# First batch of an attention and Fourier-mixing kernel: order of loads, turning, folds and normalising rearranged

## The chip, the cores and the metric

The kernel runs on one core of a Trainium2 chip. The metric is the device time of one execution in microseconds (us), read as the median of several runs; lower is better. A core has five engines that each work through their own list of instructions in order: PE (TensorE, the matrix multiplier), DVE (VectorE), ACT (ScalarE), POOL (GpSimd) and SP (SyncE, which here only issues DMA transfers). They wait for one another through semaphores.

## The reference

There are two stages in float32. The first is attention inside chunks of 64 positions; the second mixes the result with a two-dimensional Fourier transform, adds it to itself, normalises every position, and sends it through a two-layer perceptron.

```python
# q, k, v: (8, 8, 576, 64); chunks of 64 positions
scores = scale * np.matmul(q_c, k_c.transpose(0, 1, 2, 4, 3))
attn = softmax(scores)
out = np.matmul(attn, v_c)
x = out.transpose(0, 2, 1, 3).reshape(B, S, H * D)      # (8, 576, 512)
mixed = np.real(np.fft.fft(np.fft.fft(x, axis=1), axis=2))
u = x + mixed
un = (u - mean(u)) / np.sqrt(var(u) + 1e-06)
ch = np.maximum(un @ w_ch1, 0.0) @ w_ch2                # 512 -> 2048 -> 512
result = u + ch
```

The weights `w_ch1` and `w_ch2` arrive as float64 bits. They are turned into float32 by bit operations on the chip ("rounding" below).

## The kernel before

**Tiles.** A tile is 128 positions (two chunks) by 512 columns. Each batch has nine chunks: four tiles named LO 0, LO 1, HI 0, HI 1, and half a tile RE, which two batches share. LO tiles hold positions in reversed order and HI tiles their mirror images, so that a sum and a difference of a LO and a HI tile ("fold") halve the Fourier work. Batch 0 is worked alone at the start by `attention_early` and `fourier_early`. Later batches are worked as side work beside the matrix products of the perceptron, which run in groups of four tiles (`mlp`). The first group begins with `up_first`, whose first product is L1064; from there on PE has a steady supply. The order of instructions within an engine is the order in which the code is written (`tc.manual_schedule()`), so each queue can be read off the code.

**Loading.** `load(n)` queues q and k of tile n on SP (those of tile 0's k on ACT), as 128 or 256 KB DMAs. `load_v(n)` queues v in four DMAs of 64 KB: POOL for tiles 0 to 2 (half of tile 0 on ACT), SP for tiles 3 and 4. Then SP issues the token tables (ten DMAs, `token_tables`), two rows of the dimension tables, the first weight piece, the cosine and sine tables and the further weight pieces.

**Attention of batch 0.** For each tile PE turns q and k (`att_T`, four 128x128 transposes each through `turn`, L350), ACT copies them to SBUF (L380, L389), PE multiplies them (`att_S`, L401), DVE takes the maximum and subtracts it (`softmax`, L414, L416), ACT exponentiates (L427), PE turns the result (`att_P`) and ACT copies it (L433), PE multiplies by v (`att_V`, L451), and DVE divides by the row sums (L464 to L468). All the turns use two PSUM buffers named "pt". `shift_early` exchanges single rows between tiles: `shift_early(0)` on POOL (L491 to L493), `shift_early(1)` on ACT (L495 to L497). `fold(0,1)` and `fold(0,NM)`, that of RE, are POOL's; `fold(0,0)` is DVE's (L523 to L548 all are lines of `fold`).

**Fourier of batch 0.** PE multiplies the folded tiles pm by the token tables (z, L837, and single-row products mid, L840), in the order 1, 0, NM. ACT and DVE copy z to SBUF (L851 to L859), PE multiplies by the dimension tables (L876), DVE adds the result to the tiles and takes statistics (L900, L903, L655, L656). ACT makes the reciprocal root (L659 and L660, a logarithm and an exponential). `normed` normalises tiles 0 and 1 on ACT (L943 to L945) and 2 and 3 on DVE (L947). `turned` turns each (L350) and ACT copies it (L960). `columns(s)` forms the first part of the first four up products for tile s alone (L892).

**Rounding of the weights.** `round_weight(i)` starts piece i ("head": DVE L323 and L333, ACT L318, L321 and L315) and finishes piece i-1 ("tail": DVE L330, L331, L339). The first up products need piece 0, L1064 needs piece 1, and each further piece of four products needs the next. The argument `later` puts ACT's three steps on a list (`put_off`), to be written further down.

**Warming.** `keep_warm(k)` issues k matmuls of zeros on PE (L1280), 128x289 each.

Of the kernel before, what the change touches and what calls it, by code (L numbers as in the profile page):

```python
# [16 lines left out]
def kernel(  # L17
# [103 lines left out]
    for b in range(B):  # L121
        first.append(len(tiles))
        if b % 2 == 0:
            tiles.append((RE, b, 0))
        tiles += [(LO, 0, 1), (HI, 0, 1), (LO, 0, 0), (HI, 0, 0)] if b == 0 else [
            (what, b, i) for what in (LO, HI) for i in range(NM)
        ]
# [93 lines left out]
    def load_v(n):  # L221
        t = more_v[n - 3] if 3 <= n < first[1] else v_ring[n % 3]
        for i, (b, c) in enumerate(chunks(n)):
            for e in range(2):
                eng = nc.scalar if n == 0 and e else nc.gpsimd if n < 3 else nc.sync
# [8 lines left out]
    def token_tables(to):  # L234
# [5 lines left out]
        for c in range(2):  # L240
            j, p0 = divmod((NC - 1 - c) * CH, 128)
            for r in range(2):
                r0 = CH * c + CH // 2 * r
                nc.sync.dma_start(
# [3 lines left out]
        for r0 in (0, CH):  # L248
            nc.sync.dma_start(out=to[r0:r0 + CH // 2, NM], in_=seq_tab[1:CH:2, NM, :, 0:n])
            w = seq_tab.shape[1]  # L250
            lone = seq_tab.rearrange("p j r f -> (p j) r f")[0:2 * w + NM + 1:2 * w + NM]
            nc.sync.dma_start(out=to[r0 + CH // 2:r0 + CH // 2 + 2, NM], in_=lone[:, :, 0:n])
            nc.sync.dma_start(out=to[r0 + CH // 2 + 2:r0 + CH, NM], in_=seq_tab[4:CH:2, NM, :, 0:n])

    def load_tables():

        token_tables(early_tk)
        for i in range(2):
            nc.sync.dma_start(out=first_rest[32 + 32 * i:33 + 32 * i, 0:DM], in_=dim_tab[0:1, 1 + 2 * i, :])
# [86 lines left out]
    def turn(src):  # L346

        pt = ps_t.tile([128, 4, 128], FP32, tag="pt", name="pt")
# [5 lines left out]
    def att_T(n, which="qk"):  # L354
# [21 lines left out]
        a = qs.pop(n)  # L376
        pt = turn(lambda j: a[:, 2 * j:2 * j + 2, :].rearrange("p h d -> p (h d)"))
# [8 lines left out]
        a2 = ks.pop(n)  # L386
        pt = turn(lambda j: a2[:, 2 * j:2 * j + 2, :].rearrange("p h d -> p (h d)"))
# [3 lines left out]
        if first[1] <= n + 1 < NT:  # L391
            load(n + 1)
# [44 lines left out]

    def att_V(n):
        a, b = pT.pop(n), vs.pop(n)
# [7 lines left out]
        for j in range(NJ):  # L447
            for e in range(2):
                for c in range(2):
# [7 lines left out]
                    )  # L457
        x = xt(n)
# [19 lines left out]
        if kind(n) == HI:  # L478
            (nc.vector if n == at[HI, 0, 0] else nc.gpsimd).tensor_copy(x[:, 0:1], x[:, DM:DM + 1])
# [5 lines left out]
    def shift_early(i):  # L485
# [8 lines left out]
        else:  # L494
            nc.scalar.copy(rest, lows[0][r0])  # L495
            nc.scalar.copy(lows[0][r0], lows[0][r1])
            nc.scalar.copy(lows[0][r1], kept)  # L497
# [12 lines left out]
    def fold(b, i):  # L510

        eng = nc.vector if (b, i) == (0, 0) or b == 1 else nc.gpsimd
        if (b, i) == (0, 0):
            two = one_p.tile([128, KD, G * 128], FP32, tag="unT", name="two")
            two = two.rearrange("p k t -> p (k t)")[:, 0:2 * (HM + 1)]
        else:
            two = one_p.tile([128, 2 * (HM + 1)], FP32, tag="two", name="two")
        if i < NM:
# [3 lines left out]
            (nc.vector if (b, i) == (0, 0) else nc.gpsimd).memset(s[:, DM:DM + 1], 0.0)  # L522
# [13 lines left out]
        near, far = pmr[:, :, 0:HQ], pmr[:, :, HM:HQ:-1]  # L536
        if i < NM:
# [13 lines left out]
    def attention_early():  # L551
# [3 lines left out]
        def ready(n):  # L555
            if n == at[LO, 0, 1]:
                shift_early(0)
            if n == at[HI, 0, 1]:
                fold(0, 1)
            if n == at[HI, 0, 0]:  # L560
                fold(0, 0)
# [3 lines left out]
        att_T(lo)  # L565
        att_S(lo)
        for n in range(lo, hi + 1):
            if n < hi:
                att_T(n + 1)
            softmax(n)  # L570
            if n > lo:
                att_V(n - 1)
# [3 lines left out]
            if n in (lo, hi):  # L576
                keep_warm(1)
            att_P(n)
        shift_early(1)
        fold(0, NM)  # L580
        keep_warm(1)
        att_V(hi)
        ready(hi)
        keep_warm(6)
        round_weight(0)
        round_weight(1, parts="t")
# [231 lines left out]
    def fourier_early():  # L818
# [9 lines left out]
        mid = ps_f.tile([128, 512], FP32, tag="ff", name="mid")  # L828
        mids = [(CH * g + 1 if g else 0, CH * g + CH + 1 if g < 3 else NQ) for g in range(4)]
        order = (1, 0, NM)  # L830
# [29 lines left out]
        round_weight(1, put_off, "h")  # L860
# [20 lines left out]
        for do in put_off[:2]:  # L881
            do()
        keep_warm(3)
# [13 lines left out]
        for i in range(NM):  # L897
            y, (low, high) = early_xp[0][i], groups[0][2 * i:2 * i + 2]
            x = xt(low)
            nc.vector.tensor_tensor(out=x[:, 0:DM], in0=y, in1=x[:, 0:DM], op=ALU.add)  # L900
            means([low])
# [3 lines left out]
            if i == 0:  # L905
# [511 lines left out]
```

## Time and profile before

| | |
|---|---|
| median of 3 runs | 1079.0 us (1078.85 to 1080.7) |
| profiled execution | 1076.41 us |
| its span, first to last instruction | 1074.6 us |
| granted PE clock, mean | 1.000 |
| PE, DVE, ACT, POOL busy | 98%, 54%, 29%, 31% |
| PE busy in 0 to 10, 10 to 20, 20 to 30, 30 to 40, 40 to 50 us | 8.04, 8.29, 8.69, 9.77, 8.16 us |
| PE busy in 50 to 60, 60 to 70, 70 to 100 us | 10.00, 9.61, 30.00 us |
| share of DMA capacity in 0 to 20 us | 0.92 to 0.93 |
| scores' maximum (L414) of the five tiles starts at | 10.15, 12.90, 17.12, 20.52, 23.85 us |
| PE's waits before 55 us, the two longest sums | 1.8 us for ACT's copy of k, 1.6 us for ACT's normalising |

Times inside the execution count from the first instruction. PE's busy time includes the warming matmuls, so a high share in the first 50 us is not all work.

### The profile page before, as it was taken

Reading aid. Unit: us, or ns where it says so; the run is one execution under the profiler, and the core shown is the slowest. Engines: PE = TensorE matmul, PEld = TensorE weight load, DVE = VectorE, ACT = ScalarE, POOL = GpSimd, SP = SyncE. Lnnn points to the kernel's source line nnn. Section 1 sums busy time; section 2 is a strip of 40 time slices with the busy share of each in tenths; the row PEclk is TensorE's granted clock in tenths of the full one; section 3 lists DMA queues with packets and bytes.
Section 4 is the critical chain, followed back from the end, with each engine's and each line's share of the span. In section 5 each row is a group of like instructions: output and inputs, shape, how many; then the busy total and the mean of one; then the engine's idle time right before and its main releaser. Section 6 shows DMA issues by size and latency. Waiting matters only on the chain.

```text
span 1074.6 us, 19747 instructions
## 1 busy us (share of the span) xinstructions
PE 1054.5 (98%) x7418; PEld 840.0 (78%) x7418; DVE 578.6 (54%) x1269; ACT 311.6 (29%) x732; POOL 330.2 (31%) x475
## 2 busy tenths in 40 slices
PE   8999989999999999999999999999999999999998
PEld 6645444446888888888888888888888888888887
DVE  4798985324567465655565555745664434323411
ACT  4688563123113411323022312331133113101300
POOL 4311017573515240254124321624161401310140
PEclk9999999999999999999999999999999999999999
DMA  8767566598467546892678356945653355436232
GB/s 181 234 184 216 119 195 198 172 300 296 146 192 229 160 144 194 219 243 100 194 203 243 115 167 194 259 152 168 212 168 118 120 184 177 128 141 215 77 118 79
DMA packets 148780, 192.25 MB, mean 179 GB/s; under 512 B 68140, under 2 KB 105004, under 8 KB 141518
## 3 DMA queue, kind: packets, MB, share of 16 engines
q1 hardware_dynamic: 145036, 187.59, 57.8%
q10 hardware_dynamic: 3330, 2.76, 1.0%
q8 instruction: 59, 0.97, 0.4%
q0 software_dynamic: 320, 0.66, 0.3%
q14 instruction: 35, 0.29, 0.1%
HBM read 166.83 MB, written 24.12 MB: 178 GB/s over the span
## 4 chain that ended last, share of the span: by engine, by line
PE 78%; DMA 6%; DVE 4%; POOL 3%; ACT 3%; SPq 3%; issue 2%; POOLq 0%; DVEq 0%; ACTq 0%
PE pb L1200 21%; PE pa L1151 17%; PE pa L1200 16%; PE pb L1151 12%; PE up L1084 2%; PE pt L350 2%; PE up L1064 2%; DMA xall<-in_moe_w_ch_dram 2%; PE mix L791 2%; PE z L672 1%; DMA v<-in_v_dram 1%; PE xp L451 1%; SPq L216 1%; DMA q<-in_q_dram 1%; PE sc L401 1%
## 5 line engine op out<-in xcount | busy, mean ns | idle before, releaser
L1151 PE MATMUL pa<-unT,wa 128*128 128x256 f32 x672 | 159.9, 381 | 1.6 <-DVE wa L1159 1.6
L1151 PEld LDWEIGHTS pa<-unT,wa 128*128 128x128 f32 x672 | 126.2, 190 | 19.4 <-DVE wa L1159 2.0
L1052 POOL TENSOR_TENSOR h<-h 128x256 f32<-128x256 f32 x64 | 55.3, 871 | 231.2 <-DVE wb L1050 138.7
L1200 PE MATMUL pa<-wb,h 128*128 128x256 f32 x512 | 115.7, 380 | 0.0
L1200 PE MATMUL pb<-wb,h 128*128 128x256 f32 x512 | 114.9, 379 | 0.0
L1151 PE MATMUL pb<-wa 128*128 128x256 f32 x448 | 106.6, 381 | 0.0
L1200 PEld LDWEIGHTS pa<-wb,h 128*128 128x128 f32 x512 | 96.0, 190 | 13.0
L1200 PEld LDWEIGHTS pb<-wb,h 128*128 128x128 f32 x512 | 96.3, 190 | 12.6
L1151 PEld LDWEIGHTS pb<-wa 128*128 128x128 f32 x448 | 84.3, 190 | 11.5
L508 POOL COPY xall<-xall 1x512 f32<-1x512 f32 x28 | 17.8, 637 | 147.3 <-DVE xall L468 120.4
L1157 DVE TENSOR_TENSOR wa<-pb,wa 128x256 f32<-128x256 f32 x56 | 23.8, 424 | 69.9 <-ACT wa L1156 69.9
L1200 PE MATMUL pb<-wb,yall 128*128 128x256 f32 x256 | 58.2, 381 | 0.0
L1200 PE MATMUL pb<-wb 128*128 128x256 f32 x256 | 57.7, 379 | 0.0
L1200 PE MATMUL pa<-wb,yall 128*128 128x256 f32 x256 | 57.6, 379 | 0.0
L1105 PE MATMUL dn<-wb,h 128*128 128x512 f32 x128 | 57.5, 597 | 0.0
L1084 PE MATMUL up<-unT,wa 128*128 128x512 f32 x128 | 56.8, 595 | 0.0
L1156 ACT COPY wa<-pa 128x256 f32<-128x256 f32 x56 | 20.9, 372 | 124.0 <-PE pa L1151 81.2
L1151 PE MATMUL pa<-wa 128*128 128x256 f32 x224 | 53.9, 383 | 0.0
L1151 PE MATMUL pb<-unT,wa 128*128 128x256 f32 x224 | 52.9, 379 | 0.0
L1200 PEld LDWEIGHTS pa<-wb,yall 128*128 128x128 f32 x256 | 48.0, 190 | 6.1
L1200 PEld LDWEIGHTS pb<-wb,yall 128*128 128x128 f32 x256 | 47.7, 190 | 6.3
L1200 PEld LDWEIGHTS pb<-wb 128*128 128x128 f32 x256 | 47.6, 190 | 5.9
(265 smaller groups left out, 1766.8 us busy)
## 6 DMA issues: line engine op xcount, KB each, us to landing
wb<-s SPq DMA_DIRECT2D x56, 1024.0 KB
wa<-s SPq DMA_DIRECT2D x196, 256.0 KB
xall<-in_moe_w_ch_dram SPq DMA_DIRECT2D x22, 512.0 KB
q<-in_q_dram SPq DMA_DIRECT2D x96, 112.0 KB
k<-in_k_dram SPq DMA_DIRECT2D x96, 112.0 KB
v<-in_v_dram SPq DMA_DIRECT2D x124, 64.0 KB
yall<-in_moe_w_ch_dram SPq DMA_DIRECT2D x10, 512.0 KB
s<-wb SPq DMA_DIRECT2D x20, 256.0 KB
```

What stands on the lines that cost most here:

```text
L216: eng.dma_start(out=t[p0:p0 + np_], in_=src[b, :, c * CH:c * CH + np_, :].rearrange("h p d -> p h d"))
L350: nc.tensor.transpose(pt[:, j, :], src(j), ident)
L508: nc.gpsimd.tensor_copy(to, from_)
L791: nc.tensor.matmul(out=mix[:, cols], lhsT=zt[:, T], rhs=tab, start=(T == 0), stop=(T == 3), skip_group_check=True,)
L1052: nc.gpsimd.tensor_tensor(out=h1[:, m, hi], in0=h1[:, m, lo], in1=h1[:, m, hi], op=ALU.subtract)
L1064: nc.tensor.matmul(out=up, lhsT=w1[:, kk, m * 128:(m + 1) * 128], rhs=unT[:, kk], start=(kk == 0), stop=(kk == KD - 1), skip_group_check=True,
L1084: nc.tensor.matmul(out=up, lhsT=w1[:, kk, m * 128:(m + 1) * 128], rhs=unT[:, kk], start=(kk == 0), stop=(kk == KD - 1),)
L1105: nc.tensor.matmul(out=dn, lhsT=h1[:, m, s * 128:(s + 1) * 128], rhs=w2[:, m, :], start=(m == 0), stop=(m == KF - 1),)
L1151: nc.tensor.matmul(out=dst, lhsT=w[:, kk, r], rhs=rhs[o][:, kk], start=(o in (0, 1) and kk == 0), stop=(kk == 1), skip_group_check=True,)
L1156: nc.scalar.copy(a, dst)
L1157: nc.vector.tensor_tensor(out=b, in0=pbs[r][:, 0], in1=a, op=ALU.add)
L1200: nc.tensor.matmul(out=dst, lhsT=lhs[:, m], rhs=w[:, m], start=(o in (0, 2) and m == 0), stop=(m == HF - 1), skip_group_check=True,)
```

## The change

The tile order of batch 0 becomes RE, LO 1, LO 0, HI 1, HI 0. SP queues q and k of all five tiles, and then v of tiles 3 and 4. POOL queues v of tiles 0 to 2, the token tables and the two rows; a small copy that needs the first half of q of tile 0 stands before them. In the tile loop k is turned into a third PSUM bank ("bank") two tiles ahead and q into "pt", also issued by PE earlier (q three tiles ahead, k two), and ACT copies q before the exponentials' turn. `att_V` is split in products and scaling, and the scaling of tile n-1 is written behind the softmax of tile n. Both exchanges are POOL's, the first half of `fold(0,1)` is DVE's (with a buffer in `wb`) and its second half POOL's. `fold(0,NM)` comes before it. z is summed in the order NM, 1, 0. The tail of piece 0's rounding moves from before the copies of z to behind them, together with the head of piece 1. All four tiles are normalised on DVE, each directly followed by its turn and its columns. There are fewer warming matmuls.

```diff
@@ -122,7 +122,7 @@
             tiles.append((RE, b, 0))
-        tiles += [(LO, 0, 1), (HI, 0, 1), (LO, 0, 0), (HI, 0, 0)] if b == 0 else [
+        tiles += [(LO, 0, 1), (LO, 0, 0), (HI, 0, 1), (HI, 0, 0)] if b == 0 else [
             (what, b, i) for what in (LO, HI) for i in range(NM)
@@ -222,7 +222,7 @@
             for e in range(2):
-                eng = nc.scalar if n == 0 and e else nc.gpsimd if n < 3 else nc.sync
+                eng = nc.gpsimd if n < 3 else nc.sync
                 eng.dma_start(
@@ -241,22 +241,22 @@
                 r0 = CH * c + CH // 2 * r
-                nc.sync.dma_start(
+                nc.gpsimd.dma_start(
                     out=to[r0:r0 + CH // 2, 0:NM].rearrange("p i r f -> p (i r) f"),
...
         for r0 in (0, CH):
-            nc.sync.dma_start(out=to[r0:r0 + CH // 2, NM], in_=seq_tab[1:CH:2, NM, :, 0:n])
+            nc.gpsimd.dma_start(out=to[r0:r0 + CH // 2, NM], in_=seq_tab[1:CH:2, NM, :, 0:n])
             w = seq_tab.shape[1]
             lone = seq_tab.rearrange("p j r f -> (p j) r f")[0:2 * w + NM + 1:2 * w + NM]
-            nc.sync.dma_start(out=to[r0 + CH // 2:r0 + CH // 2 + 2, NM], in_=lone[:, :, 0:n])
-            nc.sync.dma_start(out=to[r0 + CH // 2 + 2:r0 + CH, NM], in_=seq_tab[4:CH:2, NM, :, 0:n])
+            nc.gpsimd.dma_start(out=to[r0 + CH // 2:r0 + CH // 2 + 2, NM], in_=lone[:, :, 0:n])
+            nc.gpsimd.dma_start(out=to[r0 + CH // 2 + 2:r0 + CH, NM], in_=seq_tab[4:CH:2, NM, :, 0:n])
...
         for i in range(2):
-            nc.sync.dma_start(out=first_rest[32 + 32 * i:33 + 32 * i, 0:DM], in_=dim_tab[0:1, 1 + 2 * i, :])
+            nc.gpsimd.dma_start(out=first_rest[32 + 32 * i:33 + 32 * i, 0:DM], in_=dim_tab[0:1, 1 + 2 * i, :])
@@ -343,9 +343,9 @@
-    def turn(src):
-
-        pt = ps_t.tile([128, 4, 128], FP32, tag="pt", name="pt")
+    def turn(src, pt=None):
+
+        pt = ps_t.tile([128, 4, 128], FP32, tag="pt", name="pt") if pt is None else pt
         for j in range(4):
@@ -373,8 +373,15 @@
             return
-        a = qs.pop(n)
-        pt = turn(lambda j: a[:, 2 * j:2 * j + 2, :].rearrange("p h d -> p (h d)"))
+        q_out(n, pair_turned(qs.pop(n)))
+        k_out(n, pair_turned(ks.pop(n)))
+        if first[1] <= n + 1 < NT:
+            load(n + 1)
+
+    def pair_turned(a, pt=None):
+        return turn(lambda j: a[:, 2 * j:2 * j + 2, :].rearrange("p h d -> p (h d)"), pt)
+
+    def q_out(n, pt):
         t = one_p.tile([128, 2 * NJ, CH + 1], FP32, tag="qT", name="qT")
@@ -383,13 +390,11 @@
         qT[n] = t
-        a2 = ks.pop(n)
-        pt = turn(lambda j: a2[:, 2 * j:2 * j + 2, :].rearrange("p h d -> p (h d)"))
+
+    def k_out(n, pt):
         t = one_p.tile([128, NJ, 128], FP32, tag="kT", name="kT")
...
         kT[n] = t.rearrange("p j (c t) -> p (j c) t", c=2)
-        if first[1] <= n + 1 < NT:
-            load(n + 1)
@@ -435,7 +440,13 @@
+    xps = {}
+
     def att_V(n):
+        att_V_products(n)
+        att_V_scaled(n)
+
+    def att_V_products(n):
         a, b = pT.pop(n), vs.pop(n)
@@ -455,6 +466,10 @@
                     )
+        xps[n] = xp
+
+    def att_V_scaled(n):
+        xp = xps.pop(n)
         x = xt(n)
@@ -476,7 +491,7 @@
         if kind(n) == HI:
-            (nc.vector if n == at[HI, 0, 0] else nc.gpsimd).tensor_copy(x[:, 0:1], x[:, DM:DM + 1])
+            (nc.vector if n < first[1] else nc.gpsimd).tensor_copy(x[:, 0:1], x[:, DM:DM + 1])
         elif kind(n) == RE:
@@ -492,9 +507,9 @@
         else:
-            nc.scalar.copy(rest, lows[0][r0])
-            nc.scalar.copy(lows[0][r0], lows[0][r1])
-            nc.scalar.copy(lows[0][r1], kept)
+            nc.gpsimd.tensor_copy(rest, lows[0][r0])
+            nc.gpsimd.tensor_copy(lows[0][r0], lows[0][r1])
+            nc.gpsimd.tensor_copy(lows[0][r1], kept)
@@ -509,17 +524,19 @@
-        eng = nc.vector if (b, i) == (0, 0) or b == 1 else nc.gpsimd
+        eng = nc.vector if b == 0 and i < NM or b == 1 else nc.gpsimd
         if (b, i) == (0, 0):
...
             two = two.rearrange("p k t -> p (k t)")[:, 0:2 * (HM + 1)]
+        elif (b, i) == (0, 1):
+            two = wb[:, 0:2 * (HM + 1)]
         else:
...
             low, high = xt(at[LO, b, i]), xt(at[HI, b, i])
-            (nc.vector if (b, i) == (0, 0) else nc.gpsimd).memset(s[:, DM:DM + 1], 0.0)
+            (nc.vector if b == 0 else nc.gpsimd).memset(s[:, DM:DM + 1], 0.0)
             eng.tensor_tensor(out=s[:, 0:DM], in0=low[:, 0:DM], in1=high[:, 0:DM], op=ALU.add)
@@ -534,6 +551,8 @@
         near, far = pmr[:, :, 0:HQ], pmr[:, :, HM:HQ:-1]
+        if (b, i) == (0, 1):
+            eng = nc.gpsimd
         if i < NM:
@@ -553,37 +572,52 @@
         def ready(n):
+            att_V_scaled(n)
             if n == at[LO, 0, 1]:
                 shift_early(0)
-            if n == at[HI, 0, 1]:
-                fold(0, 1)
-            if n == at[HI, 0, 0]:
-                fold(0, 0)
+            if n == at[LO, 0, 0]:
+                shift_early(1)
+                fold(0, NM)
+            for i in range(NM):
+                if n == at[HI, 0, i]:
+                    fold(0, i)
             if n + 3 > hi:
...
-        att_T(lo)
+        turned_q = {lo: pair_turned(qs.pop(lo))}
+        pair_turned(ks.pop(lo), bank)
+        q_out(lo, turned_q.pop(lo))
+        k_out(lo, bank)
         att_S(lo)
+        turned_q[lo + 1] = pair_turned(qs.pop(lo + 1))
+        pair_turned(ks.pop(lo + 1), bank)
+        q_out(lo + 1, turned_q.pop(lo + 1))
+        k_out(lo + 1, bank)
+        turned_q[lo + 2] = pair_turned(qs.pop(lo + 2))
         for n in range(lo, hi + 1):
-            if n < hi:
-                att_T(n + 1)
             softmax(n)
             if n > lo:
-                att_V(n - 1)
                 ready(n - 1)
...
                 att_S(n + 1)
-            if n in (lo, hi):
+            else:
                 keep_warm(1)
+            if n + 2 <= hi:
+                q_out(n + 2, turned_q.pop(n + 2))
             att_P(n)
-        shift_early(1)
-        fold(0, NM)
-        keep_warm(1)
-        att_V(hi)
+            if n + 2 <= hi:
+                pair_turned(ks.pop(n + 2), bank)
+                k_out(n + 2, bank)
+            else:
+                keep_warm(1)
+            if n + 3 <= hi:
+                turned_q[n + 3] = pair_turned(qs.pop(n + 3))
+            elif n + 3 == hi + 1:
+                load(hi + 1)
+            att_V_products(n)
         ready(hi)
-        keep_warm(6)
+        keep_warm(3)
         round_weight(0)
-        round_weight(1, parts="t")
@@ -825,9 +859,9 @@
         z += [more[:, k] for k in range(2)]
-        mid = ps_f.tile([128, 512], FP32, tag="ff", name="mid")
+        mid = bank.rearrange("p j t -> p (j t)")
         mids = [(CH * g + 1 if g else 0, CH * g + CH + 1 if g < 3 else NQ) for g in range(4)]
-        order = (1, 0, NM)
+        order = (NM, 1, 0)
         for i in order:
@@ -857,7 +891,7 @@
                 nc.scalar.copy(z4[0:1, 2, r:r + 1], chunk_order(from_))
-        round_weight(1, put_off, "h")
+        round_weight(1, put_off)
         to = zr[:, :, 0].rearrange("p t (r i) -> p t r i", r=2)
@@ -878,9 +912,7 @@
         idle[0] = mid
-        for do in put_off[:2]:
-            do()
-        keep_warm(3)
+        keep_warm(2)
         yield
@@ -898,27 +930,22 @@
             nc.vector.tensor_tensor(out=x[:, 0:DM], in0=y, in1=x[:, 0:DM], op=ALU.add)
+            if i == 1:
+                normed(0, 1)
+                turned(0, 1)
+                columns(1)
             means([low])
...
             nc.vector.tensor_tensor(out=x[:, DM:DM + 1], in0=y[:, 0:1], in1=x[:, DM:DM + 1], op=ALU.add)
-            if i == 0:
-                normed(0, 0)
-            if i == 1:
-                turned(0, 1)
-                columns(0)
+            normed(0, 2 * i)
+            turned(0, 2 * i)
+            columns(2 * i)
             means([high])
-            if i == 0:
-                normed(0, 1)
-                turned(0, 0)
-                keep_warm(1)
-        put_off[2]()
-        columns(1)
-        normed(0, 2)
-        turned(0, 2)
+            put_off.pop(0)()
+        put_off.pop(0)()
         normed(0, 3)
         turned(0, 3)
-        columns(2)
         columns(3)
@@ -938,7 +965,7 @@
         mean, rstd = sts.pop(n)
-        if g == 1 or g == 0 and s < 2:
+        if g == 1:
             shift_ = sm_p.tile([128, 1], FP32, tag="shift", name="shift")
@@ -1261,10 +1288,9 @@
             load(n)
-            if n < 3:
-                load_v(n)
-        load_v(3)
-        load_v(4)
+        nc.gpsimd.tensor_copy(zr[0:1, 0, 0, 0:1], start[0:1, 4 * DM:4 * DM + 1])
+        for n in range(first[1]):
+            load_v(n)
         load_tables()
@@ -1273,6 +1299,7 @@
         early_xp = [ps_f.tile([128, 512], FP32, tag="ff", name="early_xp") for _ in range(2)], None
+        bank = ps_f.tile([128, 4, 128], FP32, tag="ff", name="bank")
```

## The prediction

> **What bounds the kernel now.** I read busy shares first, then the table of windows, then the first 52 us engine by engine.
>
> ```profile
> PE 1054.5 (98%) x7418; PEld 840.0 (78%) x7418; DVE 578.6 (54%) x1269; ACT 311.6 (29%) x732; POOL 330.2 (31%) x475
> ```
> ```profile
> 10.00:20.00 10.00, 8.29 (x203) 6.59 (x195) 5.83 (x15) 6.40 (x13) 0.00 (x0) 1.00 0.93 192
> 40.00:50.00 10.00, 8.16 (x51) 6.46 (x50) 8.88 (x21) 8.95 (x31) 0.00 (x0) 1.00 0.57 132
> 50.00:60.00 10.00, 10.00 (x35) 5.30 (x35) 9.14 (x19) 8.48 (x14) 0.00 (x0) 1.00 0.77 239
> 70.00:100.00 30.00, 30.00 (x186) 15.35 (x185) 27.93 (x54) 25.44 (x44) 5.08 (x4) 1.00 0.72 203
> ```
> From 50 us on TensorE is full (30.00 of 30.00); before, it has gaps, and some of its work is warming matmuls. The change touches only what precedes the first product of `up_first` (L1064); after it, every engine has the same instructions in the same order. So the change is worth the shift of that one start, 51.49 us:
>
> ```profile
> 22.70 0.69 PE L401 MATMUL sc<-kT,qT 64*64 64x64 f32 x32
> 33.49 0.76 PE L837 MATMUL z<-wb,pm 128*128 128x289 f32 x2
> 37.09 0.34 PE L840 MATMUL mid<-wb,pm_rest 64*1 64x65 f32 x8
> 48.33 1.04 PE L350 MATMUL pt<-ident,un 128*128 128x128 f32 x8
> 51.49 1.88 PE L1064 MATMUL up_a<-unT,wa 128*128 128x512 f32 x4
> ```
> ```profile
> 23.85 0.68 DVE L414 TENSOR_REDUCE mx<-sc 128x8 f32<-128x512 f32 x1
> 29.61 1.23 DVE L523 TENSOR_TENSOR sum<-xall 128x512 f32<-128x512 f32 x1
> 33.25 0.16 DVE L548 TENSOR_TENSOR pm<-pm,sign 128x1 f32<-128x1 f32 x1
> 40.04 0.69 DVE L900 TENSOR_TENSOR xall<-early_xp,xall 128x512 f32<-128x512 f32 x1
> 47.74 0.55 DVE L947 TENSOR_SCALAR un<-xall,st,rstd 128x512 f32<-128x512 f32 x1 [0.35 <-ACT rstd L660]
> 50.08 0.68 DVE L339 TENSOR_TENSOR wa<-wa,power 128x512 f32<-128x512 f32 x1
> ```
> Start and length stand first; a bracket tells the wait. Milestones: last score maximum 23.85, last fold 33.41, z done 37.43, first residual add 40.04, last normalisation 48.29, first up product 51.49. Piece 1 of the weights (rounding ends L339, 50.76) is only 0.7 early, so VectorE is nearly as critical as TensorE.
>
> ```profile
> 20.75 0.60 POOL L491 COPY first_rest<-xall 1x512 f32<-1x512 f32 x1 [12.56 <-DVE xall L468]
> 28.76 0.72 POOL L530 TENSOR_TENSOR two<-xall 64x256 f32<-64x256 f32 x1
> 33.27 0.20 POOL L548 TENSOR_TENSOR pm_rest<-pm_rest,sign 64x1 f32<-64x1 f32 x1
> ```
> POOL idles 12.56 us before its first exchange, then folds (0,1) and (0,NM). Filling that idle is what the change tries with the table loads.
>
> **What the Trainium skill says.** "SBUF — State Buffer", section "SBUF: two separate sides": a DVE instruction with two SBUF inputs and a POOL instruction lock each other out of a shared port pair. The trace agrees: the fold's add took 1.23 us with POOL folding beside it, and the same add of the next batch, at 117.39 with POOL idle, 0.69. "DMA: Bandwidth & Descriptors", section "SWDGE vs HWDGE vs iDMA": GpSimd's and SyncE's DMAs feed different queues, between which an engine takes turns. The trace shows nothing against it: v loads from POOL landed by 12.8 us while q and k were still landing until 18.4. Its section "Anatomy of one DMA — SWDGE (gpsimd) path" gives 2.0 us plus bytes/436e3, an estimate of 2.15 us for 64 KB; the trace's median was 5.7 from issue to landing under load, and I use that. "TensorE: Matmul & The Clock Gate", Part 1: after an idle window of about 3.4 us the clock halves. Here PEclk stays 1.00; the first eight warming matmuls took 0.82 us and later ones 0.49.
>
> **The change, part by part.**
>
> *Tile loop.* Before, q, k and exponential share two "pt" buffers; the last three tiles are 3.3 us apart (17.12, 20.52, 23.85). With k in a third bank and q turned three tiles ahead, TensorE's own work remains, start to start: S 0.62, P 0.50, k 0.50, q 0.50, V 0.70 = 2.8 us; VectorE has 0.69+0.75+1.25 = 2.7. I take 2.7 to 2.9 for the last two distances, and 3.4 for that to the third tile (4.2 before, 12.90 to 17.12), which holds the first in-order V. Last maximum: 22.15 (−1.7). Bytes are unchanged, and DMA share is 0.93 here; tables now compete with q and k, so I put k of the last tile at 19 to 20 us (before 18.4), hardly late for its turn.
>
> *Folds.* Between the scaling of tiles 3 and 4, VectorE gains the first half of fold (0,1): 0.14+0.06+1.23+0.56+0.14+0.61 = 2.7, partly in its 1.44 us wait. From 22.15: maximum and subtraction 1.5, scaling 1.25, this 2.6, scaling 1.2, fold (0,0) 3.75 = 32.45 (−0.95).
>
> *POOL and the queues.* SyncE loses 12 table issues (4.9 us, 21.62 to 26.5), so weights start that much earlier; ACT loses two v issues. POOL gains a tiny copy that waits for the first half of q (4.41); behind it stand all v loads. The first of tile 0 then lands near 4.46+5.7 = 10.2, the last near 12 to 13, for a first V at about 14.5: hidden. POOL issues 12 v loads (0.62 each, from 4.46 after the copy that waits for q), then 10 table loads and 2 rows. With eight outstanding and 5.7 us to landing, 24 need three rounds: 4.46 + 16/8 × 5.7 + 8 × 0.55 = 20.3; I take 20.5, with 18 (SyncE's tables landed in 3 us) and 23 as ends. The last table lands some 4 us after its issue, 24 to 25, for a z that starts at 27.9: hidden up to 3 us. Behind the DMAs stand six exchanges at 0.68 (three were ACT's), fold (0,NM) 4.7 and half of fold (0,1) 1.9: done 31.4. ACT is relieved of 1.9 us, worth nothing: it was idle from 29.3 to 33.8.
>
> *z.* Order NM, 1, 0. At 20.5, (NM) runs from 27.9, (1) from 30.2, (0) from 32.8: done 35.2 (−2.2). But now the rest of piece 0's rounding and the start of piece 1's stand between the z copies and the first add: 0.33+0.60+0.61+0.33+0.60 = 2.5 us of VectorE; before, only L323 and L333 of piece 1, 0.77, stood there, and the others filled the wait for z. VectorE's two long and two short z copies, in turn with ACT's, end 1.2 after z (0.42+0.41+0.22+0.22, as from 37.85 to 39.35 before, less one wait): 36.4, plus 2.5 = first add 38.9 (−1.1). ACT's three steps on piece 0 (0.72+0.72+0.61 from 32.8) end at 34.85, when its first z copy can start; below z they cost nothing, and each 0.1 later would cost 0.1.
>
> *Normalising.* For tiles 0 and 1, ACT's 0.19+0.29+0.81 is replaced by 0.55 on VectorE. But the written order makes each tile a closed ring: normalise 0.55, turn 0.65, ACT copy 0.57, logarithm 0.33, exponential 0.23, plus hand-overs 0.1 = 2.43; the next tile's logarithm is queued on ACT behind the copy, which waits for TensorE. Add to first normalisation 2.2, three rings 7.3, the last 0.55: 10.1, against 8.25 before, where statistics ran ahead. Last normalisation: 48.99 (+0.7).
>
> *Tail.* Before 3.20 from there to L1064: two tiles' turns, copies and eight columns. Now one tile: 48.99 + turn 0.65 + copy 0.57 + columns 4×0.23 + hand-overs 0.2 = 51.3; piece 1's rounding takes 0.33+0.60+0.61+0.33+0.62 = 2.5, ready 51.48. First product 51.58 (−0.6).
>
> Sum: −1.1 + 1.8 − 0.6 = +0.1 us. The warming matmuls removed stood in idle; weights issued earlier by SyncE are not needed earlier. The profiled run was 1076.41 (span 1074.6 and 1.8 around it): 1076.5 becomes 1079.1 on the scale of the median 1079.0.
>
> **Rivals.**
>
> 1. Late POOL (slower). In the sum, POOL's done time and VectorE's fold meet at the start of z(0). Each microsecond by which POOL is free after 20.5 shifts everything: at 22.2 I get +1.9, at 23 about +2.8. From 22.6 on it decides "slower". For: DMA share 0.93, small table rows, software descriptors; against: SyncE needed only 4.3 us to issue all ten. Time: 1081.5.
> 2. The front counts in full (faster). VectorE's two fold adds meet POOL only exchanging rows and take 0.69 instead of 1.23 (1.1 less), POOL is free near 19, and the 1.8 us of piece 0's rounding (0.60+0.61+0.60) slip into waits for z as before (1.7 less): 0.1−2.8 = −2.7. For: both costs are avoidable ones, by the rows at 117.39 and 35.81. Against: in the written order that rounding comes after the copies. Time: 1076.3.
> 3. TensorE's clock falls. Between warming and the first turn some 2.5 us are empty; if the clock halves, three turns and columns take 0.5 to 1 us more each: +2. The gap is below the skill's window; PEclk never fell before. Time: 1081.
> 4. The order doesn't do what it says: q turned ahead stands in TensorE's queue before V, and waits for DMA; the loop keeps 3.3 us. Then the 1.7 gain is gone: +1.0, 1080.1, inside the range.
>
> **How the numbers follow.** About 2.2 us, 0.2%, can be told from no change. Balance near zero (with rival 4): 0.49. Rival 1: 0.23; rival 3: 0.08; rival 2: 0.20. So faster 0.20, same 0.49, slower 0.31. Likeliest time 1079.1; its own range is 1077.3 to 1080.8, and with POOL's ends and the rivals 1076.3 to 1082.3.
>
> **What would show it.** Right: last maximum near 22.2, last fold 32.5, first add 38.9, normalisations 2.4 apart on VectorE each waiting for ACT's exponential, first up product 51.6, later windows unchanged. POOL's first exchange after 22 shows rival 1; PEclk below 1.00 after 40 shows rival 3; a first add before 37.5 shows rival 2; maxima 3.3 apart show rival 4. I am wrong in kind if time moves after the first up product.

## The result, and the profile after

The changed kernel took 1087.76 us in the median of 4 runs (1086.27 to 1088.87), the kernel before 1079.83 us beside it (4 runs, 1078.85 to 1080.7): a ratio of 1.0073 with a 95% interval of 1.0053 to 1.0092. The profiled execution took 1086.27 us, with a span of 1084.5 us against 1074.6 before. It is slower, by about 8 us, where no measurable change was forecast. The profile of before is one of its quick executions, 1076.41 us, so the spans differ by 9.9 us and the medians by 7.9.

The table of windows (the columns are window, length, busy time of PE, PEld (TensorE's weight loads), DVE, ACT and POOL, granted PE clock, DMA share, GB/s; the view prints shares above 1 too):

```profile
10.00:20.00 10.00, 7.30 (x195) 6.10 (x194) 5.33 (x15) 6.45 (x14) 6.64 (x13) 1.00 1.22 220
40.00:50.00 10.00, 6.96 (x31) 5.35 (x29) 8.42 (x19) 4.13 (x21) 0.00 (x0) 0.79 0.43 108
50.00:60.00 10.00, 8.36 (x33) 7.27 (x34) 5.31 (x12) 6.02 (x14) 0.00 (x0) 0.50 0.17 52
70.00:100.00 30.00, 30.00 (x185) 15.44 (x184) 26.04 (x50) 26.14 (x44) 4.74 (x5) 1.00 0.64 172
```

The last column but two is what to read first: TensorE ran at half its clock from the middle of the 40s until past 60 us. The busy share hides it, because a matmul at half clock counts as busy for nearly twice as long. The timeline of PE shows where it began and what it did:

```profile
18.08 0.63 PE L350 MATMUL pt<-ident,start 128*128 128x128 f32 x4 [1.58 <-DMA start<-in_q_dram]
42.23 1.14 PE L1307 MATMUL bank<-warm 128*128 128x289 f32 x4
45.34 0.67 PE L350 MATMUL pt<-ident,un 128*128 128x128 f32 x4 [1.98 <-DVE un L974]
48.56 1.06 PE L350 MATMUL pt<-ident,un 128*128 128x128 f32 x4
59.38 3.62 PE L1091 MATMUL up_a<-unT,wa 128*128 128x512 f32 x4
```

The warming matmuls end at 43.36 us and the first normalised tile arrives 1.98 us later. The next turn takes 1.06 us instead of 0.67, and the first four up products (L1091, L1064 of before) 3.62 instead of 1.88. The whole start on DVE, and POOL's last load and first exchange:

```profile
23.23 0.68 DVE L419 TENSOR_REDUCE mx<-sc 128x8 f32<-128x512 f32 x1
26.24 0.24 DVE L479 TENSOR_SCALAR rd<-early_xp 128x4 f32<-128x4 f32 x2 [1.54 <-PE early_xp L462]
35.32 0.42 DVE L567 TENSOR_TENSOR pm<-pm,sign 128x1 f32<-128x1 f32 x1
42.42 0.69 DVE L932 TENSOR_TENSOR xall<-early_xp,xall 128x512 f32<-128x512 f32 x1
54.31 0.55 DVE L974 TENSOR_SCALAR un<-xall,st,rstd 128x512 f32<-128x512 f32 x1 [2.24 <-ACT rstd L694]
```
```profile
22.36 0.50 POOL L259 DMA_DIRECT2D first_rest<-in_dim_tab_dram  x1 [0.35 <-DMA wb<-in_seq_tab_dram]
23.02 0.60 POOL L506 COPY first_rest<-xall 1x512 f32<-1x512 f32 x1
```

The milestones, before and after: last maximum 23.85 and 23.23; POOL's first exchange 20.75 and 23.02; last fold ends 33.41 and 35.74; first add 40.04 and 42.42; first up product 51.49 and 59.38. So of the 9.9 us of span, 2.4 are lost up to the first add, 5.5 from there to the first up product (16.96 instead of 11.45), and 2.0 behind it; 1.7 of these are the first four products at half clock.

### The profile page after: what moved, and what is told of

It is laid out like the page before. It is cut to its first block, busy times and chain, and to the rows that moved or that the text cites. A ratio compares the mean times of both kernels' runs of the same rounds, so it can differ in the third digit from the quotient of the medians.

```text
span 1084.5 us, 19732 instructions
## 1 busy us (share of the span) xinstructions
PE 1060.4 (98%) x7408; PEld 844.1 (78%) x7408; DVE 582.0 (54%) x1277; ACT 308.0 (28%) x723; POOL 336.6 (31%) x487
## 4 chain that ended last, share of the span: by engine, by line
PE 83%; DMA 7%; DVE 4%; ACT 2%; SPq 2%; issue 1%; POOL 0%; DVEq 0%; ACTq 0%
PE pb L1227 20%; PE pa L1178 17%; PE pa L1227 15%; PE pb L1178 13%; PE up L1111 4%; PE pt L350 3%; PE dn L1132 2%; PE up L1091 2%; PE mix L825 2%; PE z L706 1%; DMA k<-in_k_dram 1%; PE xp L462 1%; SPq L216 1%; PE sc L406 1%; DMA out_dram<-o 1%
```

## The experiments

Each kernel ran beside the kernel before on the same chip, at different times and on different chips; "above before" is the difference of the two medians. Milestones are from the profiled execution of each, one of several; "add to up" is from first add to first up product. "Half clock" is the time up to 70 us in which the trace's clock record of that execution stands at 0.50.

| kernel | median, us | above before | ratio to before (95%) | last fold | add to up | half clock |
|---|---|---|---|---|---|---|
| before | 1077.7 to 1079.8 | | | 33.41 | 11.45 | none |
| after | 1087.76 | 7.9 | 1.0073 (1.0053 to 1.0092) | 35.74 | 16.96 | 45.8 to 62.9 |
| e1_warm | 1087.43 | 9.2 | 1.0082 (1.0069 to 1.0095) | 37.59 | 13.50 | 20.3 to 27.1 |
| e2_tables_sp | 1082.82 | 4.6 | 1.0039 (1.0021 to 1.0057) | 34.43 | 17.27 | 44.1 to 61.2 |
| e3_warm_tables_sp | 1080.77 | 2.5 | 1.0024 (1.0014 to 1.0033) | 35.93 | 13.50 | 19.1 to 22.5 |
| e4_norm_as_before | 1082.98 | 4.7 | 1.0049 (1.0037 to 1.0061) | 34.95 | 10.80 | none |
| e5_before_no_warm | 1081.78 | 3.5 | 1.0034 (1.0018 to 1.0050) | 33.09 | 13.86 | 45.9 to 52.7 |
| e8_before_ring | 1079.82 | 1.5 | 1.0012 (1.0003 to 1.0022) | 34.05 | 12.40 | none |
| e9_before_loads | 1078.25 | -0.1 | 1.0002 (0.9991 to 1.0014) | 34.57 | 11.46 | none |
| e6_front_only | 1076.63 | -1.7 | 0.9993 (0.9983 to 1.0004) | 33.16 | 11.51 | none |
| e7_gap_filled | 1084.64 | 6.5 | 1.0048 (1.0028 to 1.0068) | 37.99 | 12.40 | 20.9 to 24.3 |
| e10_round_in_fold | 1077.17 | -1.0 | 0.9991 (0.9982 to 1.0000) | 34.08 | 11.51 | none |
| e12_q_behind_v | 1083.62 | 5.9 | 1.0050 (1.0036 to 1.0065) | 36.92 | 12.40 | 21.0 to 24.4 |
| e11_best_q_behind_v | 1076.19 | -1.5 | 0.9989 (0.9977 to 1.0002) | 33.33 | 11.51 | none |
| e13_tables_sp | 1079.86 | 1.5 | 1.0016 (1.0008 to 1.0024) | 33.26 | 12.40 | none |
| e14_tables_pool | 1078.36 | 0.0 | 1.0006 (0.9993 to 1.0020) | 37.31 | 11.52 | 21.2 to 24.6 |

**Warming, tables, and the normalising part.** There are three theories of the loss: the fallen clock; the ring of normalising, turning and copying; and the loads in POOL's queue.

e1, more warming matmuls (e3 has the same, with e2's edit):

```diff
-        keep_warm(2)
+        keep_warm(5)
...
             turned(0, 2 * i)
+            keep_warm(1)
             columns(2 * i)
+            keep_warm(1)
...
```

> The kernel after the change with more warming matmuls: five instead of two behind the mix, and one behind each turn and each group of columns in the normalising part. Clock theory (TensorE is too idle between 43 and 58 us, its clock halves, and this costs 4.3 us before the first up product and 2.0 in it): the granted clock is 1.00 in every window, the distance between normalisations falls from 3.6 to 2.5 us, the first up product starts near 55.1 instead of 59.4, span near 1078.5. Ring theory (the closed ring of normalising, turning, copying and logarithm is what costs; the clock is a side effect): distances stay at 3.6 or grow by 0.5, span 1084 to 1086. Queue theory (POOL's table loads cost all): first add stays at 42.4 and the span hardly moves.

From 40 to 70 us the clock is 1.00 and add to up falls by 3.5 us, but the median does not move: in this profile the tile loop is late instead, last fold 37.59. TensorE stands empty there for 3.13 us in the middle of a product with v (the reason is under e12), and the clock is at half from 20.3 to 27.1 us. The warming in the ring also stands on the path (13.50 where e7 later has 12.40). So the clock theory holds for its stretch and its sum fails, because the clock can fall in a second place, the tile loop.

e2, token tables and rows on SP:

```diff
-                nc.gpsimd.dma_start(
+                nc.sync.dma_start(
...
```

> The kernel after the change with the ten token tables and two rows issued by SyncE again. Queue theory (twelve more DMAs keep POOL busy until 22.9 us, and this delays exchanges, folds, z and first add by 2.4 us): POOL's first exchange at 20.5 to 21, when the scaled tile is ready, or earlier, first add at 39.5 to 40.5 instead of 42.4; the clock still falls, so the distance between normalisations stays 3.6; span near 1082. Clock theory alone: the same clock loss and a gain of at most 2.5. If the lateness of the first add is VectorE's own (rounding of the weights between the copies of z and the add), it stays above 41.5.

The profile shows the earlier first add at 41.03, less early than expected, and a fallen clock. The 17 executions say more. Nine have a mean clock of 0.995 to 0.998 and a median of 1080.38 us, eight have 0.989 to 0.991 and 1086.40. Same kernel, same instructions: as far as the mean clock tells, the gap (1.99 us in the profile, which is one of the eight) sometimes lets the clock fall and sometimes not, and the fall costs 6.0 us.

> Both edits: more warming matmuls in the normalising part, and tables on SyncE again. If the two causes are separate, their gains add: span near 1076, first up product near 52.5, clock 1.00. If one of them is only a consequence of the other (a later first add lets the clock fall, or the fallen clock makes the late add matter), the gain is that of the larger one alone, span near 1078.5.

1080.77 is 6.7 below e1, which differs only in the tables, so they cost more than the 2.4 I had given them; e1's stop of 3.13 us is part of that. The first up product (56.12) is 3.6 later than expected: even with the tables on SP, PE waited 1.76 us for q here, and the clock was at half from 19.1 to 22.5 us.

e4, the block of `fourier_early` from the adds on, as before (with the ACT branch of `normed` and the three warming matmuls):

```diff
-        if g == 1:
+        if g == 1 or g == 0 and s < 2:
...
-            normed(0, 2 * i)
-            turned(0, 2 * i)
-            columns(2 * i)
+            if i == 0:
+                normed(0, 0)
...
```

> The kernel after the change with the normalising part as before (tiles 0 and 1 on ACT, statistics written ahead of the turns, three and one warming matmuls). Clock theory: TensorE's longest gap is 1 us as before, the clock stays at 1.00, first add to first up product takes 11.5 us as before instead of 17.0; first up product near 53.9, span near 1077.5. If the clock falls because of the longer attention or z part, it falls here too, and the span stays above 1081.

Add to up is 10.80, but the median stays 5 above before. In this profile the start of the up products is 0.9 us late, and 6.2 us are lost behind it: in pieces, among them the windows 160 to 165 and 215 to 220 us, where the clock is 0.66. These falls are not this edit's: between 150 and 175 us the clock falls for 3.4 or 6.8 us in every profile but those of before and e1, also in those of quick kernels like e6 and e11, and near 215 us also in e5 and e7. What they cost, and what else e4 loses there, is not settled.

**The clock and the ring alone, in the kernel before.** e5 removes its four warming matmuls of the normalising part, e8 gives it the changed normalising part, e9 the changed loads.

```diff
-        keep_warm(3)
         yield
...
-                keep_warm(1)
```

> The kernel before the change with only the four warming matmuls of the normalising part removed; nothing else differs. Clock theory: TensorE then has no work from 41.6 to 44.3 us, and its clock falls to half by about 46; turns and columns (6 us of TensorE's time) and the first products run at half speed: first up product at 53 to 56 instead of 51.5, span 3 to 6 us longer than before. Rival: a gap of 2.7 us is too short for the clock to fall; first up product and span as before.

PE of e5:

```profile
45.37 0.66 PE L350 MATMUL pt<-ident,un 128*128 128x128 f32 x4 [2.51 <-ACT un L943]
47.97 1.06 PE L891 MATMUL up_a<-unT,wa 128*128 128x128 f32 x4
53.12 0.71 PE L891 MATMUL up_a<-unT,wa 128*128 128x128 f32 x4
55.01 1.88 PE L1062 MATMUL up_a<-unT,wa 128*128 128x512 f32 x4
```

Nothing but idle time was added, and the columns take 1.06 us until 51 and 0.71 from 53. The loss is 3.5 us in the median. In the profile the clock's part is 2.4 (add to up 13.86 for 11.45); the first add is 1.1 late for another reason, a first weight piece for which DVE waited 1.05 us. This is the clock mechanism shown by itself.

```diff
-            if i == 0:
-                normed(0, 0)
+            normed(0, 2 * i)
+            turned(0, 2 * i)
+            columns(2 * i)
...
```

> The kernel before the change with only the normalising part of the change (all four tiles on VectorE, each turned and its columns formed at once, two warming matmuls). First add stays at 40.0. If ring and fallen clock are what the change loses in this part, first add to first up product takes 16 to 17 us instead of 11.5 and the span grows by 6 to 7.5; if the clock stays up it takes 12.7 to 13.5 and the span grows by 1.5 to 2; if the later start of this part is needed for the loss, nothing grows.

```profile
42.38 1.13 PE L1273 MATMUL mid<-warm 128*128 128x289 f32 x4
43.75 0.63 PE L350 MATMUL pt<-ident,un 128*128 128x128 f32 x4 [0.24 <-DVE un L940]
53.22 1.98 PE L1057 MATMUL up_a<-unT,wa 128*128 128x512 f32 x4
```

The same ring, but here the first tile comes 0.24 us after the warming, not 1.98. The clock stays, add to up is 12.40, and the median is 1.5 above before. So the ring costs 0.95 us, and it does not let the clock fall of itself. The gap does, and the gap is there after the change because 2.6 us of weight rounding stand on DVE ahead of the first add (39.84 to 42.42; 0.8 in e8), while the mix does not wait for them.

```diff
             load(n)
-            if n < 3:
-                load_v(n)
-        load_v(3)
-        load_v(4)
+        nc.gpsimd.tensor_copy(zr[0:1, 0, 0, 0:1], start[0:1, 4 * DM:4 * DM + 1])
+        for n in range(first[1]):
+            load_v(n)
...
-                nc.sync.dma_start(
+                nc.gpsimd.dma_start(
...
```

> The kernel before the change with only the loads of the change (q and k of all tiles first, all early v on POOL behind the copy that waits for q, token tables and two rows on POOL). Queue theory: POOL's first exchange moves from 20.8 to 22 to 23, v of tiles 3 and 4 land 2 to 3 us later because the tables share the DMA engines with them; the first add is 1.5 to 2.5 later and so is the end (span 1076 to 1077.5); the clock stays at 1.00. Rival: the loads are hidden, first add 40.0 to 40.5.

The profile has the expected delay (exchange 22.12, first add 41.20, first up product 52.66), but the median does not: no cost that could be told.

**The gap, q, and the tables.** e7 fills only the gap.

```diff
-        keep_warm(2)
+        keep_warm(6)
```

> The kernel after the change with six warming matmuls instead of two behind the mix, in the 2.0 us in which TensorE waits for the first normalised tile; nothing else differs. Clock theory, narrowed: that one gap lets the clock fall. Then the granted clock stays at 1.00 through the ring, first add to first up product takes 12.4 to 12.7 us instead of 17.0, and the median falls from 1087.8 to 1080.5 to 1082.5; what remains against before is the later fold and the ring. If the short gaps in the ring (0.7 us, two in each turn) let the clock fall on their own, it falls here too, later, and the median stays above 1084.

```profile
20.25 0.63 PE L350 MATMUL pt<-ident,start 128*128 128x128 f32 x4 [2.69 <-DMA start<-in_q_dram]
23.23 1.11 PE L350 MATMUL pt<-ident,ex 128*128 128x128 f32 x4
44.48 3.08 PE L1307 MATMUL bank<-warm 128*128 128x289 f32 x12
47.60 0.63 PE L350 MATMUL pt<-ident,un 128*128 128x128 f32 x4
57.07 1.98 PE L1091 MATMUL up_a<-unT,wa 128*128 128x512 f32 x4
```

Add to up is 12.40, as in e8: the clock is settled for this stretch. The median fell by 3.1 only (1.4 when each is set against the kernel before beside it, which the scatter hides), between the two expectations, and the first two lines show what took its place. PE waits 2.69 us for q, with a product with v behind it, and now the clock falls here: turns take 1.11 us instead of 0.66, and the last fold ends at 37.99. The seven executions again make two groups: three with a mean clock of 0.997 or 0.998 and 1081.2 to 1082.2 us, as the clock theory expected, and four with 0.994 or 0.995 and 1084.6 to 1087.9; the profile is one of the four.

```diff
+            att_V_products(n)
             if n + 3 <= hi:
                 turned_q[n + 3] = pair_turned(qs.pop(n + 3))
             elif n + 3 == hi + 1:
                 load(hi + 1)
-            att_V_products(n)
```

> The gap-filled kernel (after the change, six warming matmuls behind the mix) with one more edit: q of the tile after the next two is turned behind the product with v, not ahead of it. If q turned ahead is what stalls TensorE's queue (1.6 us after the change, 2.7 in the gap-filled profile, both waits for q's DMA with v products behind), the maxima of tiles 3 and 4 come at 20 to 21 and 23 to 24 and the median is 1 to 2 below 1084.6, with no run above 1086. If the late DMAs themselves bound the loop, whichever queue waits, maxima and median stay within 0.7.

1.0 us in the median, which is within the scatter (0.6 against the kernels before), with an unclear profile: the maxima come at 22.48 and 26.26. TensorE no longer waits for q, but stands empty for 1.37 us in the middle of q's turn, all of which had landed by 18.9, and the clock falls.

This stop is TensorE's wait for its own next instructions, as the traces read. It comes after 217 matmuls, whatever stands there: a turn in e12, the product with v in e1, e2, e4, e6 and e10 (and after 216 in e9). Each time TensorE goes on 1.3 to 1.6 us after a 16 KB DMA of the queue that the profile calls "instruction" has ended (19.21 in e12). The next such place, in the changed kernel and e4, is 124 matmuls on; with their weight loads and eight semaphore instructions that is 256 instructions, or 64 bytes each. The profile counts these DMAs among the transfers of the core's 16 DMA engines, as it does the loads; the stop is 0.3 us long in e6 and 3.1 in e1. The late DMAs look like the larger part of what the tile loop loses. By the semaphore events of the trace the last piece of k lands at 22.6 us here, against 18.4 before and 20.6 in the changed kernel.

e13 is e12 with e2's edit.

> The kernel with gap filled and q behind v, and now also tables and rows on SyncE. If the tables on POOL's queue are the rest of the loss: last k lands at 18.5 to 20 instead of 22.6, last fold at 34 to 35 instead of 36.9, median 1079 to 1080.5 instead of 1083.6; what is left against before is the ring, about 1 us, and the later fold. If the tables are not it, the median stays above 1082.

DVE and PE of e12, and then of e13:

```profile
26.26 0.68 DVE L419 TENSOR_REDUCE mx<-sc 128x8 f32<-128x512 f32 x1
36.76 0.16 DVE L567 TENSOR_TENSOR pm<-pm,sign 128x1 f32<-128x1 f32 x1
43.76 0.69 DVE L932 TENSOR_TENSOR xall<-early_xp,xall 128x512 f32<-128x512 f32 x1
20.70 0.65 PE L350 MATMUL pt<-ident,start 128*128 128x128 f32 x3 [1.37 <-issue]
22.34 1.11 PE L350 MATMUL pt<-ident,ex 128*128 128x128 f32 x4
```
```profile
22.70 0.68 DVE L419 TENSOR_REDUCE mx<-sc 128x8 f32<-128x512 f32 x1
33.10 0.16 DVE L567 TENSOR_TENSOR pm<-pm,sign 128x1 f32<-128x1 f32 x1
39.86 0.69 DVE L932 TENSOR_TENSOR xall<-early_xp,xall 128x512 f32<-128x512 f32 x1
18.07 0.72 PE L350 MATMUL pt<-ident,start 128*128 128x128 f32 x4
19.35 0.66 PE L350 MATMUL pt<-ident,ex 128*128 128x128 f32 x4
```

The last k lands at 18.3, everything up to the first add is 3.6 to 3.9 us earlier (0.8 of it stands already at the first tile's maximum, before any table is loaded), and the median falls by 3.8 (4.4 against the kernels before). The two ratios lie clear of each other. What the tables cost is thus two things in one, transfers that land later, q, k and TensorE's instructions, and the clock that falls while TensorE stands empty; no run parts them.

**A version that beats before?** e6 undoes tables, normalising part and place of the rounding, and keeps tile loop, split fold and order of z:

```diff
         round_weight(0)
+        round_weight(1, parts="t")
...
-        round_weight(1, put_off)
+        round_weight(1, put_off, "h")
...
```

> The kernel after the change with three parts undone: tables on SyncE, the rest of piece 0's rounding before the copies of z, the normalising part as before. What remains is the tile loop, the split fold and the order of z. If the three parts are all that costs, the first add comes at 39 to 39.5 (41.5 with the rounding between), the first up product at 50 to 51, and the kernel is as fast as before or up to 1.5 us faster; if the rounding in front of the copies delays them as much as it delayed the add, first add stays at 41 and the kernel is 0.5 to 1.5 slower than before.

As fast as before, but the first add is still at 39.88. The reason shows when the table's fold column is set against the first adds: in the changed kernel, e1 to e4, e6, e7, e9 and e13 the add comes 6.60 to 6.72 us after the last fold, as before (6.63), whatever the order of z (e8 6.77, e12 6.84; e5 8.06, with its late weight piece). e10 moves the head of piece 0's rounding into that fold:

```diff
         eng.tensor_tensor(out=pmr[:, 1], in0=near, in1=far, op=ALU.subtract)
+        if (b, i) == (0, 0):
+            round_weight(0)
...
-        round_weight(0)
         round_weight(1, parts="t")
```

> The front-only kernel with one more edit: piece 0's first rounding steps stand inside the last fold on VectorE, so that ACT's three steps run beside the fold. In every kernel so far the first add came 6.6 to 6.7 us after the last fold ended, whatever the order of z or of the rounding. If VectorE and ACT bound that stretch with piece 0's rounding, it shrinks to 4.2 to 4.8 here (the fold ends 0.7 later), the first add comes at 38 to 39, and the median is 1 to 2 us below that of the front-only kernel (1076.6), and below before. If the copies of z and the mix bound it, it stays at 6.6 and the end moves 0.7 later.

DVE of e10:

```profile
32.05 0.41 DVE L323 TENSOR_SCALAR power<-yall 128x512 uint32<-128x512 uint32 x1
33.71 0.37 DVE L569 TENSOR_TENSOR pm<-pm,sign 128x1 f32<-128x1 f32 x1
36.57 0.42 DVE L887 COPY zf<-z 128x256 f32<-128x256 f32 x1
38.76 0.69 DVE L936 TENSOR_TENSOR xall<-early_xp,xall 128x512 f32<-128x512 f32 x1
```

From the fold's end (34.08) to the add it now takes 4.68 us, and the first up product starts at 50.27. So the rounding of piece 0 through ACT bounded that stretch. The median, 1077.17, did not show it against e6. e11 adds e12's edit to e10:

> The kernel with rounding in the fold and one more edit: q turned behind the product with v. If the q wait (1.2 us here) stands on the path, last fold at 33 to 33.5 instead of 34.1, first up product at 49 to 49.7, median 0.5 to 1 below 1077.2; if q's turn is needed as soon as that anyway, no change.

The first up product starts at 49.45, 2.0 us before the old one; the median is 1076.19 against 1077.68 of before, ratio 0.9989. The interval reaches 1.0002, so it is the best of the kernels run and not shown to be better than before.

e14 puts e11's tables on POOL.

> The kernel with rounding in the fold and q behind v (1076.2), and the tables and rows on POOL as in the change. If the tables delay q, k and v wherever the tile loop is the changed one: last k at 20 to 22.5 instead of 18.6, last fold at 35 to 37 instead of 33.3, median 1079 to 1081. If it is only the loads with the rest of the change, the median stays within 0.7 of 1076.2, as the loads alone did in the kernel before.

The last k lands at 22.4 us, PE waits 2.59 us for q, the clock is at half from 21.2 to 24.6, and the last fold ends 4.0 later than e11's, the first up product 3.9 later. The median is 2.2 us higher, or 1.5 against the kernels before, a little less than expected, and the two intervals overlap. So the tables delay the start in both kernels in which the tile loop is the changed one; in the median this is clear in e12 against e13 alone.

## Why the prediction was wrong

Two terms of the sum failed. The gap in TensorE's work before the first normalised tile was put at nothing, as too short for the clock, and it cost about 6 us. The loads of the last tiles were put at "hardly late", and the whole gain of the tile loop went with what came late.

- **What bounds.** That the change is worth the shift of the first up product held for most of it: 7.9 of 9.9 us of span. The rest came behind it, which the prediction called wrong in kind; 1.7 of it is the clock again.
- **Tile loop.** "k of the last tile at 19 to 20 us, hardly late for its turn": this step failed first in order of time. It landed at 20.6, and at 22.6 in e12. PE waited 1.58 us for q and 0.34 for k, and the last maximum came at 23.23 instead of 22.15. From the second maximum to the last it took 10.97 us, where 9.25 were forecast and 10.95 were taken before. Another 1.54 us of DVE's wait, at 26.24, stand before the scaling of tile 3: PE stopped for 1.07 us in that tile's product with v, whose four loads had landed by 23.5, until 1.7 us after an instruction DMA (22.72 to 24.00). No term of the sum had TensorE waiting for instructions. Rival 4 named the wait for q and sized its loss in the loop right, but left out the tables and the instructions.
- **POOL and the folds.** POOL was free at 22.9 instead of 20.5, at the late end of the range given, and done with its folds at 34.6 instead of 31.4 (the terms given add up to 31.2). I treated this as POOL's own lateness only. In the last fold DVE waited 0.51 us for it. The larger cost was what its queue's transfers did to q, k and the instructions: 3.8 us in e12 against e13, with the clock's fall that came of it. The folds' two adds took 0.69 us each with POOL folding beside them, as rival 2 had it, not the 1.23 of the sum, but other steps took longer (L547 0.98 and 0.79 for 0.56). The last fold ended at 35.74, 3.3 later than the 32.45 forecast.
- **z and first add.** The stretch from fold to add was sized right: 6.45 forecast, 6.68 measured. The 2.2 us that the order of z was to gain are no gain, as 6.63 before shows: the sum gave them back as rounding.
- **Normalising and tail.** 12.7 forecast, 12.40 with the clock up (e7, e8, e12, e13), against 11.45 before. Right.
- **TensorE's clock.** Rival 3 had the mechanism and the place, but I gave it 2 us and a chance of 0.08, on the ground that the gap of 2.5 us "is below the skill's window". "TensorE: Matmul & The Clock Gate", Part 1, names about 3.4 us of idle. Here 1.98 us were enough, in all four executions of the changed kernel by their mean clock of 0.987 to 0.994, and about as much in eight of seventeen of e2. The price is 6.0 us between the two groups of e2; in profiles it is 4.6 in the ring (16.96 against 12.40 in e7) and 1.7 in the first products. That the clock would fall in the tile loop too, as it did in e1, e3, e7, e12 and e14, no rival had.

The steps from the changed kernel to before, each set against the kernel before beside it: 7.9 us after the change, 6.5 with the gap filled, 5.9 with q behind v, 1.5 with the tables back, of which the ring explains 0.95. Only the step of the tables is clear of the scatter in the medians. That of the gap, 1.4, is not: e7 has the later tile loop and its fallen clock in it, so the clock's price rests on e2, e5 and the stretch from add to up. That the changed kernel's own tile loop kept its clock, in the one execution that was profiled, and e7's did not, is chance as far as the runs tell. Why e9's delay does not show in its median, and what e4 loses behind its first up product, stays open.

## What to carry to other kernels

Filling an idle queue with transfers isn't free when the DMA engines are at 0.93 of their capacity: ask which load the next waiting engine needs, and what is now in its way; TensorE's instructions are among these loads. Before a stage is lengthened on one engine, look at how long TensorE is empty meanwhile: a gap of 2 us between two stages cost about 6 us here, and a few more matmuls of zeros kept the clock up. Then look for the next such gap: in five profiles the clock fell in the tile loop, where TensorE waited for loads or instructions. When an operand is turned further ahead on an engine that works in order, its wait moves in front of work that was ready; what that alone costs in the median was not shown here. And read the clock of the whole start, not of the stage that was changed.

## What was not expected of the hardware

- The clock falls after gaps shorter than 3.4 us, and not always. It fell at most 0.6 us after gaps of 1.98 us (after), 1.99 (e2) and 2.51 (e5) before the first normalised tile, and during or up to 1.3 us after gaps of 1.37 (e12), 1.76 (e3), 2.59 (e14), 2.69 (e7) and 3.13 us (e1) in the tile loop. It did not fall after 1.58 us in the tile loop of the changed kernel, 2.16 in e4, or 1.06 and 1.12 in e9 and e6. So the length of the gap alone does not decide it. For the tile loop this is read from the order of events; no run fills those gaps.
- By the clock records of the traces, every stretch at half clock that ends before the last 5 us of an execution lasted 3.41 us or a whole multiple: 3.41, 6.83 or 17.07.
- Once down, it stayed at 0.50 through a ring in which PE was busy 8.36 of 10 us (50 to 60 us), and came back at 62.87, 3.5 us into the up products and 5.4 after the ring's last gap.
- TensorE stops at fixed places of its instruction list while the next 16 KB of instructions are on their way. All stops above 1 us (after, e1, e4, e12) are in kernels with the tables on POOL, where the profile's DMA share in 10 to 20 us is 1.22 (after) and 1.23 (e12); with the tables on SP, e13 has a share of 1.00 and no such stop above 0.3 us.
